# A range check's flag moved amid the last steps of an attention tail, with two banks for the turned sums and new scheduler settings

**Chip, cores, metric.** One core of one Trainium2 chip. The metric is the device time of one execution in microseconds (us); each comparison also runs the kernel before on the same chip.

## The reference

Two independent halves, written side by side into one output of 2048 x 1280 in bfloat16. The spectral half (A) multiplies a 2-d FFT by weights and transforms back. The attention half (B):

```python
H = 32; Dh = D // H                       # D = 640, Dh = 20, S = 2048
q, k, v = ...                             # from x @ wqkv
scores = jnp.einsum("bhqd,bhkd->bhqk", q, k) * Dh ** -0.5
p = _softmax(scores, axis=-1)
o = jnp.einsum("bhqk,bhkd->bhqd", p, v)
return (o, heads side by side) @ wo
```

## The kernel before

The kernel is made by a scheduler in Python. It walks through a simulated time with estimated durations (`occupy(engine, ns)`) and lays down one order of instructions for each engine. That order is then fixed; on the chip, semaphores decide when each instruction runs.

Attention is cut into 32 units (4 query blocks x 8 groups of 4 heads). Scores go by tiles of 128 x 512 through TensorE (PE). The exponentials are shared: ScalarE (ACT) takes groups of 3 and 2 tiles, VectorE (DVE) computes pairs of tiles by itself in 8 steps. The fast program skips the usual maximum of the softmax, so at its end it checks ranges (smallest and largest denominator, largest V) and makes a flag; every engine loads the flag and either jumps over a slow, safe program or runs it.

The V maxima, found as V is ready, and the last unit's steps (cut):

```python
def vmax(self):
    ...
    self.P.add("dve", lambda e: e.tensor_reduce(o, in_, AX.X, ALU.max, apply_absolute_value=True), ...)
    self.occupy("dve", 800.0)             # the scheduler's estimate

# tail_pe: turn the expanded reciprocals back by a matmul with the identity; all four in bank 4
    l, idf, o = self.rb[:, c], self.idf, ps[:, 4, c]
    self.P.add("pe", lambda e: e.matmul(o, l, idf, start=(qb == 0), stop=True, ...), ...,
               **({"w": [("ps", 4)]} if qb == 0 else {"pw": [("ps", 4)]}), name="tail_spread")
    ...
    ok = (qb == 0 or end) and (g == -1 or self.n_norm == 31)      # partial sums of the output projection

def tail_norm(self, qb):                  # normalise a quarter of the last unit
    b, osb, o = self.ps[:, 4, c], self.osb[:, c], self.OTn[:, NG - 1, c]
    self.P.add("dve", lambda e: e.tensor_tensor(o, osb, b, ALU.mult), ...)

def emit_flag(self):                      # called when all else is laid down
    # dve: csum (max over units), cv (max of V), f0, f1, f2 (comparisons)
    # pe: fsum (sum over partitions);  dve: fmin, flag

# every engine, at the end of its own list
    eng.wait_ge(flag semaphore)
    bad = eng.value_load(flag, min_val=0, max_val=3)
    with eng.If(bad > 0): ...             # the slow program
    # SyncE: wait for all output stores
```

Of the kernel before, what the change touches and what calls it, by code (L numbers as in the profile page):

```python
# [13 lines left out]
ALU = mybir.AluOpType  # L14
AX = mybir.AxisListType
# [218 lines left out]
NG = 8  # L234
# [1136 lines left out]
PE_LAT = 170.0  # L1371
# [13 lines left out]
class FK(KB):  # L1385
# [82 lines left out]
    def setup_B(self):  # L1468
        P = self.P
# [6 lines left out]
        kq[np.arange(128) % 32 < 20, 2] = 1.0  # L1476
        kqd = self.nc.inline_tensor(kq, self.prefix + "kq")
# [613 lines left out]
    def tail_pe(self):  # L2091
# [13 lines left out]
        for qb in range(4):  # L2105
            if self.tail_n.get(("e", qb), 1e18) <= self.now:
                del self.tail_n["e", qb]
                c = slice(qb * 128, (qb + 1) * 128)
                l, idf, o = self.rb[:, c], self.idf, ps[:, 4, c]
                self.P.add("pe", lambda e: e.matmul(o, l, idf, start=(qb == 0), stop=True, skip_group_check=True), r=[("rbl", qb), ("idf",)],  # L2110
                           **({"w": [("ps", 4)]} if qb == 0 else {"pw": [("ps", 4)]}), name="tail_spread")
                t = self.occupy("pe", self.pe_dur(300.0, "f"), PE_LAT)
                self.dve_urgent.append((t, lambda qb=qb: self.tail_norm(qb)))
                return True
# [16 lines left out]
        if self.tail_op:  # L2131
            qb, half, g = self.tail_op[0]
            ok = (qb == 0 or end) and (g == -1 or self.n_norm == 31)
            if qb == 0 and g == -1:

                bank = self.TAIL_BANK[0, half]
                ok = (self.u_act == 32 and self.x_pair is None and self.x_bank is None and not any(J.pe for J in self.jobs)
                      and self.bank_own.get(bank) is None and self.bank_t.get(bank, 0.0) <= self.now)
                if ok:
                    self.bank_own[bank] = "tail"  # L2140
            if ok:
                self.tail_op.pop(0)
                self.tail_mm(qb, half, g)
                return True
        return False

    def tail_rec(self):
        rin, rc, rb, ps = self.rin, self.rc, self.rb, self.ps
        P, mm = self.P, self.mm
# [3 lines left out]
        for h in range(2):  # L2153
# [5 lines left out]
            self.tail_n["e", 2 * h] = self.tail_n["e", 2 * h + 1] = t  # L2159
        self.now -= 800.0  # L2160
        m, both = mm[:, 62:64], self.rr.rearrange("p (c e) -> p c e", c=2)
        self.dve_urgent.append((self.now + 2000.0, lambda: (P.add("dve", lambda e: e.tensor_reduce(m, both, AX.X, ALU.max), r=[("rin",), ("rc",)], pw=[("mm",)], name="sums"), self.occupy("dve", 150.0))))
        self.at(self.now + 2000.0)

    def tail_norm(self, qb):
        c = slice(qb * 128, (qb + 1) * 128)
        b, osb, o = self.ps[:, 4, c], self.osb[:, c], self.OTn[:, NG - 1, c]
        self.P.add("dve", lambda e: e.tensor_tensor(o, osb, b, ALU.mult), r=[("osb",), ("ps", 4)], w=[("OTl", qb)], pw=[("OT", NG - 1)], name="tail_nrm")
        self.tail_n["n", qb] = self.occupy("dve", 270.0, 100.0)
# [141 lines left out]
    def vmax(self):  # L2311
# [8 lines left out]
        self.occupy("dve", 800.0)  # L2320
# [34 lines left out]
    def run(self):  # L2355
# [93 lines left out]
        self.emit_flag()  # L2449

    def emit_flag(self):
        P = self.P
        c, mm, fl = self.cert, self.mm, self.flagt
        ps = self.ps

        both = mm.rearrange("p (u c) -> p c u", c=2)
        P.add("dve", lambda e: e.tensor_reduce(c[:, 0:2], both, AX.X, ALU.max), r=[("mm",)], w=[("c", 0)], name="csum")
        P.add("dve", lambda e: e.tensor_reduce(c[:, 2:3], self.vmx, AX.X, ALU.max), r=[("vmx",)], w=[("c", 2)], name="cv")
        P.add("dve", lambda e: e.tensor_single_scalar(c[:, 3:4], c[:, 0:1], 65000.0, ALU.is_le), r=[("c", 0)], w=[("c", 3)], name="f0")
        P.add("dve", lambda e: e.tensor_single_scalar(c[:, 4:5], c[:, 1:2], 2.0 ** -6, ALU.is_le), r=[("c", 0)], w=[("c", 4)], name="f1")  # L2460
        P.add("dve", lambda e: e.tensor_single_scalar(c[:, 5:6], c[:, 2:3], 2.0 ** 60, ALU.is_le), r=[("c", 2)], w=[("c", 5)], name="f2")
        o1 = self.ones1
        P.add("pe", lambda e: e.matmul(ps[0:1, 7, 0:3], o1[:, 0:1], c[:, 3:6], start=True, stop=True),
              r=[("c", 3), ("c", 4), ("c", 5), ("ones1",)], w=[("ps", 7)], name="fsum")
        P.add("dve", lambda e: e.tensor_reduce(fl[0:1, 1:2], ps[0:1, 7, 0:3], AX.X, ALU.min), r=[("ps", 7), ("c", 5)], w=[("fl", 1)], name="fmin")
        fi = fl.bitcast(mybir.dt.int32)[0:1, 0:1]
        self.flag_task = P.add("dve", lambda e: e.tensor_single_scalar(fi, fl[0:1, 1:2], 127.5, ALU.is_lt), r=[("fl", 1)], w=[("fl", 0)], name="flag")
        self.flag = fi

# [8 lines left out]
def bass_concat_heads__spectral_gfnet__softmax_full_mha__prompt_kernel(  # L2478
# [11 lines left out]
    fast = FK(nc, arena, *args, cfg=dict(LEAD=32, T_A=600000.0, WARM_SHARE=0.43, RUN=1, PVQ=12, WIN=1400.0, T_X=30000.0, AHEAD=45e3, T_RB=9000.0, SKIP=0, ALONE=500.0, PVB=10, PTB=6, WARMUP=10))  # L2490
# [32 lines left out]
```

## Time and profile before

| | before |
|---|---|
| time, median of 6 runs | 858.4 us (857.6 to 858.7) |
| profiled execution | 856.3 us |
| first exponential starts | 10.50 us |
| last exponential ends | 841.35 us |
| last output add ends | 849.97 us |
| flag done | 851.02 us |

The span falls into the exponentials, where background work of half A and the projections is fitted in, and the tail behind them. The prediction shows the views of ScalarE and VectorE. TensorE's timeline of the tail shows the other partner (columns: start, length, engine, line, operation, operands, count, and in brackets the idle time before it and what ended it):

```profile
843.16 0.95 PE L2099 MATMUL ps<-arena 128*128 128x4 f32 x8
844.99 0.71 PE L2110 MATMUL ps<-arena 128*128 128x128 f32 x4
846.09 0.49 PE L2110 MATMUL ps<-arena 128*128 128x128 f32 x2 [0.38 <-DVE arena L2168]
846.95 0.49 PE L2110 MATMUL ps<-arena 128*128 128x128 f32 x2 [0.38 <-DVE arena L2168]
847.28 1.79 PE L2087 MATMUL ps<-arena 128*128 128x320 bf16 x12
```

L2099 sums the denominators, L2110 are the four turns, in fp32 (eight instructions in these rows, two for each turn), L2087 the twelve closing matmuls, in bf16 (one instruction each). The third turn waits for the first normalisation (0.38 us), the second normalisation waits for the third turn (0.58), the fourth turn waits for that (0.38): with its guard by bank, the kernel makes a ladder of the one bank. The output stores' line says how long they take from issue to landing:

```profile
DMA to landing us min/median/max: 1.8/1.9/1.9
```

### The profile page before, as it was taken

How to read it: one execution, taken by the hardware profiler on the slowest of the kernel's cores; microseconds unless marked ns; L12 is line 12 of the kernel's file. 1: busy time of each engine (PE TensorE's matmuls, PEld its weight loads, DVE VectorE, ACT ScalarE, POOL GpSimd, SP SyncE). 2: the span in 40 equal slices, each digit the busy share in tenths (PEclk: the TensorE clock that was granted, in tenths of full speed). 3: DMA queues.
4: the chain of work that ended last, by engine and by line, in shares of the span. 5: the costliest groups of instructions: out<-in, count | busy, mean ns of one | idle time of the engine just before them, and what ended most of it. 6: DMA issues, size and time to landing. Idle time of an engine off the chain costs nothing.

```text
span 856.3 us, 18371 instructions
## 1 busy us (share of the span) xinstructions
PE 796.4 (93%) x7802; PEld 277.2 (32%) x7828; DVE 760.6 (89%) x1475; ACT 830.3 (97%) x738; POOL 2.9 (0%) x8
## 2 busy tenths in 40 slices
PE   8999999999899999998899988888899999999995
PEld 4333323324223333332223432222333332333333
DVE  3577599999998999999998899999999889899983
ACT  6999999999999999999999999999999999999993
POOL 1000000000000000000000000000000000000000
PEclk9999999999999999999999999999999999999999
DMA  7520000000321000010101000001002111011201
GB/s 244 124 58 14 2 14 15 15 15 15 120 66 36 15 14 15 11 41 14 51 14 44 16 3 13 13 14 42 14 13 63 37 35 31 8 37 45 75 15 64
DMA packets 34461, 31.97 MB, mean 37 GB/s; under 512 B 13893, under 2 KB 28485, under 8 KB 34373
## 3 DMA queue, kind: packets, MB, share of 16 engines
q1 hardware_dynamic: 33796, 30.21, 11.7%
q8 instruction: 62, 1.02, 0.5%
q10 hardware_dynamic: 576, 0.52, 0.2%
q14 instruction: 27, 0.21, 0.1%
HBM read 24.97 MB, written 5.50 MB: 36 GB/s over the span
## 4 chain that ended last, share of the span: by engine, by line
ACT 56%; DVE 30%; PE 11%; issue 1%; POOL 0%; DVEq 0%; POOLq 0%
ACT arena L1783 56%; DVE arena L227 5%; DVE arena L1857 5%; PE ps L1766 3%; DVE arena L1253 3%; DVE arena L1897 2%; DVE arena L1901 2%; DVE arena L1525 2%; DVE arena L1904 2%; PE ps L1952 2%; PE ps L1581 2%; DVE arena L2318 1%; DVE arena L1893 1%; DVE arena L1895 1%; DVE arena L1899 1%
## 5 line engine op out<-in xcount | busy, mean ns | idle before, releaser
L1783 ACT ACTIVATE arena<-ps 128x1536 bf16<-128x1536 f32 x727 | 823.8, 1349 | 6.0 <-PE ps L1766 4.8
L1766 PE MATMUL ps<-arena 32*128 32x512 bf16 x2048 | 312.1, 384 | 35.6 <-ACT arena L1783 21.8
L1952 PE MATMUL ps<-arena 128*32 128x512 bf16 (+3 forms) x2048 | 192.9, 385 | 0.7 <-DVE arena L227 0.4
L1857 DVE TENSOR_SCALAR arena<-ps 128x512 uint16<-128x512 f32 x232 | 157.4, 684 | 10.2 <-PE ps L1766 9.8
L1766 PEld LDWEIGHTS ps<-arena 32*128 32x128 bf16 x2048 | 77.7, 91 | 268.5 <-ACT arena L1783 184.1
L227 DVE CAST arena<-ps 128x320 bf16<-128x320 f32 (+3 forms) x190 | 103.8, 546 | 25.0 <-PE ps L1610 11.5
L1901 DVE TENSOR_TENSOR arena<-arena 128x1024 f16<-128x1024 f16 x116 | 79.7, 687 | 1.0
L1897 DVE TENSOR_TENSOR arena<-arena 128x1024 f16<-128x1024 uint16 x116 | 79.5, 685 | 0.9
L1904 DVE TENSOR_TENSOR arena<-arena 128x1024 uint16<-128x1024 uint16 x116 | 79.3, 683 | 0.4
L1646 PE MATMUL ps<-arena 128*32 128x512 bf16 x808 | 75.4, 386 | 1.1 <-DVE arena L1972 1.1
L1952 PEld LDWEIGHTS ps<-arena 128*32 128x32 bf16 (+1 forms) x2048 | 47.4, 93 | 76.8 <-issue 63.3
L1525 DVE TENSOR_SCALAR arena<-ps,arena 128x512 bf16<-128x512 f32 x61 | 49.2, 806 | 23.6 <-PE ps L1581 14.3
L227 DVE COPY arena<-ps 128x1024 bf16<-128x1024 bf16 (+4 forms) x65 | 45.1, 697 | 14.1 <-PE ps L540 7.7
L1581 PE MATMUL ps<-arena 128*32 128x512 bf16 x640 | 53.1, 384 | 1.0 <-DVE arena L227 0.6
L1895 DVE TENSOR_SCALAR arena<-arena 128x1024 f16<-128x1024 uint16 x116 | 48.8, 421 | 1.0
L1662 PE MATMUL ps<-arena 128*32 128x512 bf16 x640 | 49.0, 382 | 0.6 <-DVE arena L227 0.4
L1893 DVE TENSOR_SCALAR arena<-arena 128x1024 uint16<-128x1024 uint16 x116 | 48.8, 421 | 0.7
L1899 DVE TENSOR_SCALAR arena<-arena 128x1024 f16<-128x1024 uint16 x116 | 48.9, 421 | 0.4
L1334 PE MATMUL ps<-arena 128*128 128x320 bf16 (+1 forms) x192 | 37.1, 302 | 0.0
L2032 PE MATMUL ps<-arena 128*128 128x320 bf16 x192 | 36.8, 302 | 0.3 <-DVE arena L227 0.3
L1610 PE MATMUL ps<-arena 128*128 128x80 bf16 (+1 forms) x320 | 32.2, 236 | 0.0
L1646 PEld LDWEIGHTS ps<-arena 128*32 128x32 bf16 x808 | 19.4, 93 | 39.1 <-issue 34.0
(74 smaller groups left out, 425.4 us busy)
## 6 DMA issues: line engine op xcount, KB each, us to landing
arena<-rscr SPq DMA_DIRECT2D x31, 256.0 KB
arena<-in_A_x_dram SPq DMA_DIRECT2D x4, 640.0 KB, 4.8
out_dram<-arena SPq DMA_DIRECT2D x4, 640.0 KB, 3.4
out_dram<-arena SPq DMA_DIRECT2D x15, 160.0 KB, 1.8
arena<-f_ciCS SPq DMA_DIRECT2D x8, 256.0 KB, 3.1
arena<-arena SPq DMA_DIRECT2D x124, 2.0 KB, 1.7
arena<-in_B_x_dram SPq DMA_DIRECT2D x3, 640.0 KB, 5.4
arena<-f_cslab SPq DMA_DIRECT2D x2, 768.0 KB, 5.2
```

The lines of the kernel that those rows point to most:

```text
L227: return eng.tensor_copy(out, in_)
L1525: return e.tensor_scalar(out, in_, m, b, ALU.mult, ALU.add)
L1581: inst = e.matmul(ps[32 * j:32 * j + 32, bank, :], self.wqkv[:, cbv, c:c + 32], r_, start=st, stop=sp, tile_position=(0, 32 * j))
L1646: i = e.matmul(ps[32 * j:32 * j + 32, 6, :], z, k, start=False, stop=False, skip_group_check=True, tile_position=(0, 32 * j))
L1766: inst = e.matmul(ps[:, bank, :], kt_[32 * j:32 * j + 32, g, kt * 128:(kt + 1) * 128], q[32 * j:32 * j + 32, :], start=True, stop=True, ti ...
L1783: self.P.add("act", lambda e: e.activation(pt, in_, AF.Exp, scale=SCALE, bias=-15.0 / LOG2E), r=[("ps", h + k) for k in range(n)], w=[("PT ...
L1857: self.P.add("dve", lambda e: e.tensor_scalar(v, in_, 1024.0 * SCALE * LOG2E, 31743.0, ALU.mult, ALU.min), r=[("ps", bank)], **({"w": [key ...
L1897: t = self.x_op(n, two, lambda e: e.tensor_tensor(b16, sh, b16, ALU.mult), [ka, kb], [kb], "x_q")
L1899: t = self.x_op(n, one, lambda e: e.tensor_scalar(a16, sh, -4.0 * X_B / 65536.0, -4.0 * X_A, ALU.mult, ALU.add), [ka], [ka], "x_l")
L1901: t = self.x_op(n, two, lambda e: e.tensor_tensor(b16, b16, a16, ALU.mult), [ka, kb], [kb], "x_h")
L1904: t = self.x_op(n, two, lambda e: e.tensor_tensor(v, v, b16, ALU.add), [kb, kv], [kv], "x_w")
L1952: inst = e.matmul(ps[32 * j:32 * j + m, 6, :], va[:, kt, 21 * h:21 * h + m], pt, start=st, stop=sp, tile_position=(0, 32 * j))
```

## The change

The intent: the flag's steps go where VectorE waits anyway, so that nothing follows the last output add; the turned sums alternate between banks 4 and 3, so that a turn and a normalisation can overlap; five settings are tuned anew. The diff, cut to its core:

```diff
+        kq[:, 4:6] = (65000.0, 2.0 ** -6)            # both limits as a tensor: one comparison for two
 # tail_pe
-                l, idf, o = self.rb[:, c], self.idf, ps[:, 4, c]
-                ... start=(qb == 0), stop=True, skip_group_check=True ... "w"/"pw": [("ps", 4)]
+                l, idf, o = self.rb[:, c], self.idf, ps[:, 4 - qb % 2, 0:128]
+                ... start=True, stop=True ... w=[("ps", 4 - qb % 2)]
+                if qb == 3:
+                    self.flag_mm()                     # now shifted by 300 around it
-            ok = (qb == 0 or end) and ...
+            ok = (qb == 0 or (end and self.tail_b is not None)) and ...
 # tail_rec, tail_norm
-            self.tail_n["e", 2 * h] = self.tail_n["e", 2 * h + 1] = t
+            if h == 0: self.tail_n["e", 0] = self.tail_n["e", 1] = t     # turns 2, 3 after norms 0, 1
+        self.flag_sums()                               # sums, csum, f0; occupy 560
+        if qb < 2: self.tail_n["e", qb + 2] = max(t, self.tail_e)
+        if qb == 3: self.flag_out()                    # fmin, flag; occupy 300
 # vmax
-        self.occupy("dve", 800.0)
+        self.occupy("dve", 760.0)
+        if kt == 15:
+            self.flag_v()                              # cv, f2; occupy 320
 # the end
-        self.emit_flag()
 # settings
-  T_A=600000.0, ... PVQ=12, ... T_X=30000.0, AHEAD=45e3, ... SKIP=0
+  T_A=560000.0, ... PVQ=10, ... T_X=25000.0, AHEAD=60e3, ... SKIP=2
```

More of the change, by code (lines that the diff above doesn't have):

```diff
@@ L2108, in tail_pe @@
                 c = slice(qb * 128, (qb + 1) * 128)
-                l, idf, o = self.rb[:, c], self.idf, ps[:, 4, c]
-                self.P.add("pe", lambda e: e.matmul(o, l, idf, start=(qb == 0), stop=True, skip_group_check=True), r=[("rbl", qb), ("idf",)],
-                           **({"w": [("ps", 4)]} if qb == 0 else {"pw": [("ps", 4)]}), name="tail_spread")
+                l, idf, o = self.rb[:, c], self.idf, ps[:, 4 - qb % 2, 0:128]
+                self.P.add("pe", lambda e: e.matmul(o, l, idf, start=True, stop=True), r=[("rbl", qb), ("idf",)],
+                           w=[("ps", 4 - qb % 2)], name="tail_spread")
                 t = self.occupy("pe", self.pe_dur(300.0, "f"), PE_LAT)
                 self.dve_urgent.append((t, lambda qb=qb: self.tail_norm(qb)))
+                if qb == 3:
+                    self.now += 300.0
+                    self.flag_mm()
+                    self.now -= 300.0
                 return True
@@ L2132, in tail_pe @@
             qb, half, g = self.tail_op[0]
-            ok = (qb == 0 or end) and (g == -1 or self.n_norm == 31)
+            ok = (qb == 0 or (end and self.tail_b is not None)) and (g == -1 or self.n_norm == 31)
             if qb == 0 and g == -1:
@@ L2148, in tail_rec @@
         rin, rc, rb, ps = self.rin, self.rc, self.rb, self.ps
-        P, mm = self.P, self.mm
+        P = self.P
         P.add("dve", lambda e: e.tensor_single_scalar(rin, ps[:, 2, 0:16], 1.0e-30, ALU.max), r=[("ps", 2)], w=[("rin",)], name="tail_max")
@@ L2158, in tail_rec @@
             t = self.occupy("dve", 350.0, 90.0)
-            self.tail_n["e", 2 * h] = self.tail_n["e", 2 * h + 1] = t
-        self.now -= 800.0
-        m, both = mm[:, 62:64], self.rr.rearrange("p (c e) -> p c e", c=2)
-        self.dve_urgent.append((self.now + 2000.0, lambda: (P.add("dve", lambda e: e.tensor_reduce(m, both, AX.X, ALU.max), r=[("rin",), ("rc",)], pw=[("mm",)], name="sums"), self.occupy("dve", 150.0))))
-        self.at(self.now + 2000.0)
+            self.tail_e = t
+            if h == 0:
+                self.tail_n["e", 0] = self.tail_n["e", 1] = t
+        self.now += 350.0
+        self.flag_sums()
+        self.now -= 1150.0
     def tail_norm(self, qb):
         c = slice(qb * 128, (qb + 1) * 128)
-        b, osb, o = self.ps[:, 4, c], self.osb[:, c], self.OTn[:, NG - 1, c]
-        self.P.add("dve", lambda e: e.tensor_tensor(o, osb, b, ALU.mult), r=[("osb",), ("ps", 4)], w=[("OTl", qb)], pw=[("OT", NG - 1)], name="tail_nrm")
-        self.tail_n["n", qb] = self.occupy("dve", 270.0, 100.0)
+        b, osb, o = self.ps[:, 4 - qb % 2, 0:128], self.osb[:, c], self.OTn[:, NG - 1, c]
+        self.P.add("dve", lambda e: e.tensor_tensor(o, osb, b, ALU.mult), r=[("osb",), ("ps", 4 - qb % 2)], w=[("OTl", qb)], pw=[("OT", NG - 1)], name="tail_nrm")
+        t = self.tail_n["n", qb] = self.occupy("dve", 270.0, 100.0)
+        if qb < 2:
+            self.tail_n["e", qb + 2] = max(t, self.tail_e)
+        if qb == 3:
+            self.now += 270.0
+            self.flag_out()
+            self.now -= 270.0
     def tail_add(self, qb, half):
@@ L2319, in vmax @@
                    r=[("V", kt, part) for part in range(4)] + [("Vones",)], pw=[("vmx",)], name="vmax")
-        self.occupy("dve", 800.0)
+        self.occupy("dve", 760.0)
+        if kt == 15:
+            self.now += 760.0
+            self.flag_v()
+            self.now -= 760.0
         return True
@@ L2448, in run, with flag_v @@
         self.sim_ns = self.now
-        self.emit_flag()
-    def emit_flag(self):
-        P = self.P
-        c, mm, fl = self.cert, self.mm, self.flagt
-        ps = self.ps
+    def flag_v(self):
+        c, vx = self.cert, self.vmx
+        self.P.add("dve", lambda e: e.tensor_reduce(c[:, 2:3], vx, AX.X, ALU.max), r=[("vmx",)], w=[("c", 2)], name="cv")
+        self.P.add("dve", lambda e: e.tensor_single_scalar(c[:, 5:6], c[:, 2:3], 2.0 ** 60, ALU.is_le), r=[("c", 2)], w=[("c", 5)], name="f2")
+        self.occupy("dve", 320.0)
@@ L2456, in emit_flag, with flag_sums @@
+    def flag_sums(self):
+        P, c, mm, rr, kq = self.P, self.cert, self.mm, self.rr, self.kq
         both = mm.rearrange("p (u c) -> p c u", c=2)
+        m, last = mm[:, 62:64], rr.rearrange("p (c e) -> p c e", c=2)
+        P.add("dve", lambda e: e.tensor_reduce(m, last, AX.X, ALU.max), r=[("rin",), ("rc",)], pw=[("mm",)], name="sums")
         P.add("dve", lambda e: e.tensor_reduce(c[:, 0:2], both, AX.X, ALU.max), r=[("mm",)], w=[("c", 0)], name="csum")
-        P.add("dve", lambda e: e.tensor_reduce(c[:, 2:3], self.vmx, AX.X, ALU.max), r=[("vmx",)], w=[("c", 2)], name="cv")
@@ L2459, in emit_flag @@
-        P.add("dve", lambda e: e.tensor_single_scalar(c[:, 3:4], c[:, 0:1], 65000.0, ALU.is_le), r=[("c", 0)], w=[("c", 3)], name="f0")
-        P.add("dve", lambda e: e.tensor_single_scalar(c[:, 4:5], c[:, 1:2], 2.0 ** -6, ALU.is_le), r=[("c", 0)], w=[("c", 4)], name="f1")
-        P.add("dve", lambda e: e.tensor_single_scalar(c[:, 5:6], c[:, 2:3], 2.0 ** 60, ALU.is_le), r=[("c", 2)], w=[("c", 5)], name="f2")
-        o1 = self.ones1
-        P.add("pe", lambda e: e.matmul(ps[0:1, 7, 0:3], o1[:, 0:1], c[:, 3:6], start=True, stop=True),
-              r=[("c", 3), ("c", 4), ("c", 5), ("ones1",)], w=[("ps", 7)], name="fsum")
@@ L2465, in emit_flag, with flag_mm @@
-        P.add("dve", lambda e: e.tensor_reduce(fl[0:1, 1:2], ps[0:1, 7, 0:3], AX.X, ALU.min), r=[("ps", 7), ("c", 5)], w=[("fl", 1)], name="fmin")
+        P.add("dve", lambda e: e.tensor_tensor(c[:, 3:5], c[:, 0:2], kq[:, 4:6], ALU.is_le), r=[("c", 0), ("kq",)], w=[("c", 3)], name="f0")
+        return self.occupy("dve", 560.0)
+    def flag_mm(self):
+        o1, c, ps = self.ones1, self.cert, self.ps
+        self.P.add("pe", lambda e: e.matmul(ps[0:1, 6, 0:3], o1[:, 0:1], c[:, 3:6], start=True, stop=True),
+                   r=[("c", 3), ("c", 5), ("ones1",)], w=[("ps", 6)], name="fsum")
+        self.occupy("pe", self.pe_dur(150.0, "f"), PE_LAT)
@@ L2466, in emit_flag, with flag_out @@
+    def flag_out(self):
+        P, fl, ps = self.P, self.flagt, self.ps
+        P.add("dve", lambda e: e.tensor_reduce(fl[0:1, 1:2], ps[0:1, 6, 0:3], AX.X, ALU.min), r=[("ps", 6)], w=[("fl", 1)], name="fmin")
         fi = fl.bitcast(mybir.dt.int32)[0:1, 0:1]
@@ L2468, in emit_flag @@
         self.flag = fi
+        self.occupy("dve", 300.0)
     def build(self):
@@ L2489, in bass_concat_heads__spectral_gfnet__softmax_full_mha__prompt_kernel @@
     arena = Arena(nc, 212832 - 64)
-    fast = FK(nc, arena, *args, cfg=dict(LEAD=32, T_A=600000.0, WARM_SHARE=0.43, RUN=1, PVQ=12, WIN=1400.0, T_X=30000.0, AHEAD=45e3, T_RB=9000.0, SKIP=0, ALONE=500.0, PVB=10, PTB=6, WARMUP=10))
+    fast = FK(nc, arena, *args, cfg=dict(LEAD=32, T_A=560000.0, WARM_SHARE=0.43, RUN=1, PVQ=10, WIN=1400.0, T_X=25000.0, AHEAD=60e3, T_RB=9000.0, SKIP=2, ALONE=500.0, PVB=10, PTB=6, WARMUP=10))
     fast.build()
```

## The prediction

> **What bounds the kernel now.** I read the page's slices and groups first, then busy time by stretch, then the timeline of the last 17 us, and last the instructions behind the flag. The groups say how long the exponentials on ScalarE (ACT) take, and how many score tiles VectorE (DVE) takes off it:
> ```profile
> L1783 ACT ACTIVATE arena<-ps 128x1536 bf16<-128x1536 f32 x727 | 823.8, 1349 | 6.0 <-PE ps L1766 4.8
> L1857 DVE TENSOR_SCALAR arena<-ps 128x512 uint16<-128x512 f32 x232 | 157.4, 684 | 10.2 <-PE ps L1766 9.8
> ```
> L1857 is the first step of the exponential that VectorE does by itself, in pairs of tiles. There are 2048 tiles (32 heads x 16 key blocks x 4 query blocks); VectorE takes 232, ScalarE the other 1816, at 823.8 / 1816 = 0.454 us each. It stands idle for only 6.0 us ahead of all 727 of them. The stretches (columns: stretch, its length, then busy us of PE, PEld, DVE, ACT and POOL, clock, DMA share, GB/s) say the same:
> ```profile
> 25.00:100.00 75.00, 73.39 (x881) 28.05 (x882) 48.21 (x82) 73.67 (x67) 0.29 (x1) 1.00 0.24 56
> 100.00:400.00 300.00, 285.44 (x2891) 96.69 (x2890) 290.43 (x566) 299.85 (x267) 0.00 (x0) 1.00 0.09 29
> 700.00:841.30 141.30, 134.68 (x1199) 45.61 (x1200) 126.29 (x253) 141.30 (x126) 0.00 (x0) 1.00 0.12 38
> ```
> From 100 to 400 us and from 700 us on, ScalarE is busy 100% of the time. So the time is three pieces: 10.5 us until the first exponential (it starts at 10.50 in ScalarE's timeline), some 831 us of exponentials to 841.3, and a tail of 15.0 us to the span's end at 856.3. Work moved between engines inside the middle piece changes nothing, unless it moves tiles between ScalarE and VectorE; an instruction saved in the tail counts in full, if it is on the tail's chain.
>
> The tail on VectorE and ScalarE, from the two timelines:
> ```profile
> 841.96 0.69 DVE L1972 COPY arena<-ps 128x512 f32<-128x512 f32 x1 [4.99 <-PE ps L1952]
> 844.15 0.18 DVE L2150 TENSOR_SCALAR arena<-ps 128x16 f32<-128x16 f32 x1 [1.49 <-PE ps L2099]
> 845.74 0.29 DVE L2168 TENSOR_TENSOR arena<-arena,ps 128x128 bf16<-128x128 f32 x1 [0.60 <-PE ps L2110]
> 846.61 0.29 DVE L2168 TENSOR_TENSOR arena<-arena,ps 128x128 bf16<-128x128 f32 x1 [0.58 <-PE ps L2110]
> 847.48 0.49 DVE L2168 TENSOR_TENSOR arena<-arena,ps 128x128 bf16<-128x128 f32 x2 [0.48 <-PE ps L2110]
> 848.29 1.68 DVE L2175 TENSOR_TENSOR arena<-ps,arena 128x320 bf16<-128x320 f32 x4 [0.33 <-PE ps L2087]
> 849.90 0.21 DVE L2457 TENSOR_REDUCE arena<-arena 128x2 f32<-128x64 f32 x1
> 850.47 0.19 PE L2463 MATMUL ps<-arena 128*1 128x3 f32 x2 [1.39 <-DVE arena L2461]
> 850.88 0.14 DVE L2467 TENSOR_SCALAR arena<-arena 1x1 int32<-1x1 f32 x1
> ```
> VectorE's steps here are short, and the bracket before nearly every one says that it waits for TensorE: the sums turned back (L2110) and the normalisation (L2168) take turns. The flag (L2457 to L2467) begins only where the last output add (L2175) ends, and ends at 850.88 + 0.14 = 851.02, 5.28 us ahead of the end. What those hold is in the lines of the flag's load, of the branch, and of the block's end:
> ```profile
> L178 DVEq TENSOR_LOAD <-arena x1: 543/543/543, 851.1 to 851.1; - x1
> L178 PEldq TENSOR_LOAD <-arena x1: 493/493/493, 851.1 to 851.1; - x1
> L179 PEldq COMPARE_BRANCH  x1: 4022/4022/4022, 851.9 to 851.9; - x1
> L168 ACTq DRAIN  x1: 80/80/80, 854.7 to 854.7; - x1
> L168 DVEq DRAIN  x1: 57/57/57, 855.3 to 855.3; - x1
> L168 PEldq DRAIN  x1: 63/63/63, 856.0 to 856.0; - x1
> ```
> All engines load the flag at the same moment and jump over the fallback program that is not run. From load to the drain behind the jump ScalarE takes 854.7 - 851.1 = 3.6 us, VectorE 4.2, TensorE 4.9; the last is the end, less 0.3 us of barrier.
>
> [...] The kernel does guard by bank: hence the waits of about 0.6 us above when all four turned sums share bank 4. [...] here 128x1 takes 0.14 us[...].
>
> **The change part by part.**
>
> First, the rest of qb=1's partial sums (an fp32 matmul) no longer stands ahead of the sum over the denominators (L2099) in TensorE's queue. The sum starts at 843.16; its input, the copy L1972, is there at 841.96 + 0.69 = 842.65. With 0.06 for the semaphore it could start at 842.71: 0.45 us earlier. But the fp32 pieces now stand behind it: the sum takes 0.81 us to issue (843.16 to 843.97), so to 843.52; then 0.53 + 0.13 + 0.53 if three of the four remaining steps come ahead of the turns, as the order of the scheduler's own estimates would have it: 844.73. VectorE's reciprocals are ready 0.45 us early, at 844.99 - 0.45 = 844.54. So the first turn starts at about 844.73, not 844.99. **Gain 0.25 us.**
>
> Second, two banks. Before, the first normalisation waits for two turns and each later one for a turn that itself waited for the one before. After: first turn 844.73 to 845.22 (0.49 us for its two instructions); VectorE does the last unit's sums, the maximum over all units and the comparison in the gap (0.18 + 0.21 + 0.15 us behind the expanding copy that ends 0.45 us earlier than 845.14, so 844.69 to about 845.25); first normalisation 845.26 (before 845.74), second 845.48 (846.61), turns 3 and 4 from 845.6 and 845.8, normalisations 3 and 4 about 846.14 and 846.36, done 846.65 (before 847.97). [...] Hence the first add starts about 848.29 - 1.09 = 847.20. The flag's last two steps (0.15 + 0.14 us, L2465 and L2467) fit before it, at 846.65 to 846.97. **Gain at the adds about 1.1 us, the first step's 0.25 included.** The adds themselves remain 1.68 us: VectorE ends at 848.88 and not at 849.97.
>
> Third, nothing is behind the adds any more: the flag is there at about 846.97, and each engine loads and jumps once its own work is over. TensorE: last matmul done about 848.0, plus 4.9, is 852.9. VectorE: 848.88 + 4.2 = 853.1. ScalarE: the last store is issued at 848.93 to 849.28 (before 850.01 to 850.36), plus 3.6, is 852.9. SyncE has to see the last store land, 1.9 us after its issue: 850.8, not on the path. Plus 0.3 for the barrier: end 853.4, 2.9 us ahead of 856.3. Of that, 1.1 is the turns and 1.8 the flag. I take **2.8 us**, as the reducing of the V maxima (0.16 + 0.14 us) moves into the middle on VectorE, where it costs next to nothing.
>
> Fourth, the settings. T_X = 25 us for 30 lets VectorE begin its tiles sooner; AHEAD = 60 for 45 us forces the K and V projections sooner; T_A = 560 for 600 us paces the spectral half faster; SKIP = 2 lets a VectorE tile pass two groups that use its rows; PVQ = 10 for 12 gates background work. All this only counts by tiles moved. One pair more on VectorE takes 2 x 0.454 = 0.91 us from ScalarE and costs VectorE 2 x 0.684 + 3 x 0.421 + 3 x 0.685 = 4.7 us. VectorE stands idle for 75 - 48.2 = 26.8 us between 25 and 100 us and for about 15 us after 700 us, so there is room for some pairs. But TensorE is busy for 73.4 of those 75 us and the projections hold the two spare banks there, and more projections forced early makes that worse. I can't work out the schedule by hand; a setting chosen anew is likelier to help. My choice: two pairs, **1.8 us**, from one pair lost to five gained.
>
> Sum: 858.3 - 2.8 - 1.8 = 853.7 us.
>
> **The rivals.** (a) The jump sets the end whatever happens: if the instruction fetches behind it, not the flag's value, are the limit and do not begin sooner, or if TensorE's 4.0 us become longer when output stores are still under way, the third step gives 0.5 us in place of 1.8: about 855.0. For it: the 4022 ns are unlike the 50 to 72 ns of the other engines' branch. Against: each engine's load stands right behind the flag (851.1 after 851.02). (b) The flag's steps amid the tail delay it: the chain L2162-L2457-comparison ahead of the first normalisation is as long as the gap, and if each dependent step costs 0.2 us plus a semaphore, the normalisations lose 0.2 to 0.4 us: about 854.0. (c) The settings hurt or help more than thought: VectorE kept off tiles by the new rule of SKIP, or TensorE congested before 100 us, gives about 856; five pairs gained gives about 851. This is the largest doubt, as nothing in the profile bounds it but VectorE's idle time.
>
> **Range and chances.** The tail's gain is 2.2 to 3.3 us, the settings' -1 to 4.5; together I hold 850.8 to 856.6 for 8 in 10. Two per cent would be 17 us, more than the whole tail of 15.0 us or than 18 pairs of tiles: faster by over 2% has a chance of 0.01, slower by over 2% 0.01 as well.
>
> **What would show each step right or wrong.** The denominators' sum should start within 0.1 us of the end of the last copy. The second normalisation should start some 0.2 us after the first, with no wait of 0.58 us ahead of it. The flag should be ready before the first output add, and the engines' loads of it should no longer stand at one moment, with VectorE's right behind its last add. From the end of the last exponential to the end of the span there should be about 12.1 us, not 15.0. Count the VectorE tiles: 236 against 232 is my guess, and 0.454 us a tile is what a different count is worth. I am wrong if the end keeps 5 us behind the last add plus a second wait, or if the exponentials' piece (10.5 to 841.3) moves by over 4 us either way.

In the trace of before an fp32 matmul of 128x320 is two instructions 0.269 us apart, so 0.538 us, and a bf16 one 0.136; put in for 0.53 and 0.13 in the first step they give the same 844.73. (The 0.06 for the semaphore is 0.05 there, from the end of the first normalisation at 846.03 to the third turn at 846.09.) The 1.09 us of the second step is the forecast move of the closing matmuls, which started at 847.28, to a place behind the flag's matmul at about 846.2.

## The result

The change takes 856.88 us in the median of 6 runs (855.87 to 860.6), the kernel before 858.4. The ratio is 0.9989 (0.9971 to 1.0007): no difference is established by these runs. (A ratio is the mean of one kernel's fast runs over the mean of the other's of the same rounds, so not quite the ratio of the medians quoted.) The gain that was forecast, 4.6 us, did not come; by the medians 1.5 us of it may have. The change's runs also spread more (855.9 to 860.6 us against 857.6 to 858.7); the section on the settings comes back to that.

The tail did what was forecast. VectorE's timeline of the kernel after:

```profile
843.26 0.69 DVE L1973 COPY arena<-ps 128x512 f32<-128x512 f32 x1 [1.93 <-PE ps L1953]
846.00 0.18 DVE L2477 TENSOR_REDUCE arena<-arena 128x2 f32<-128x32 f32 x1
846.47 0.16 DVE L2479 TENSOR_TENSOR arena<-arena 128x2 f32<-128x2 f32 x1
846.63 0.51 DVE L2174 TENSOR_TENSOR arena<-arena,ps 128x128 bf16<-128x128 f32 x2
847.50 0.51 DVE L2174 TENSOR_TENSOR arena<-arena,ps 128x128 bf16<-128x128 f32 x2 [0.36 <-PE ps L2111]
848.11 0.14 DVE L2492 TENSOR_SCALAR arena<-arena 1x1 int32<-1x1 f32 x1
848.77 1.68 DVE L2187 TENSOR_TENSOR arena<-ps,arena 128x320 bf16<-128x320 f32 x4 [0.52 <-PE ps L2088]
```

The normalisations (L2174) come in two pairs without the ladder's waits, the flag (L2492) is done at 848.25, and the last add ends at 850.45 with nothing behind it. TensorE, of the same kernel:

```profile
844.00 1.05 PE L2100 MATMUL ps<-arena 128*128 128x4 f32 x8
846.21 0.61 PE L2111 MATMUL ps<-arena 128*128 128x128 f32 x4
846.98 0.71 PE L2111 MATMUL ps<-arena 128*128 128x128 f32 x4
847.74 1.80 PE L2088 MATMUL ps<-arena 128*128 128x320 bf16 x12
```

The sum (L2100) starts 0.05 us behind the copy's end (843.95). From the last exponential's end (842.75) to the end of the span (854.87) there are 12.1 us, where before had 15.0: the forecast was 12.1 (that it is met to a tenth is luck, as point 4 of the account below says). The loads of the flag, the branches and the drains now stand apart:

```profile
L178 PEldq TENSOR_LOAD <-arena x1: 484/484/484, 848.9 to 848.9; - x1
L178 ACTq TENSOR_LOAD <-arena x1: 623/623/623, 850.9 to 850.9; - x1
L179 PEldq COMPARE_BRANCH  x1: 4122/4122/4122, 849.8 to 849.8; - x1
L168 PEldq DRAIN  x1: 63/63/63, 853.9 to 853.9; - x1
L168 ACTq DRAIN  x1: 82/82/82, 854.5 to 854.5; - x1
L168 SPq COMPARE_BRANCH  x1: 38/38/38, 854.5 to 854.5; - x1
```

TensorE jumps while VectorE still adds (its branch starts at 849.8 us, the last add ends at 850.45). ScalarE, which issues the last store, is now last (3.6 us from load to drain, as before), together with SyncE, which I had not expected; its own waits and the stores' landings say why:

```profile
SPq L191 <- DMA out_dram<-arena: 2.6, 2, 2.3
DMA to landing us min/median/max: 1.8/3.9/4.0
```

SPq L191 is SyncE's wait for the output stores (us in total, times, longest). The stores now take twice as long to land as before (3.9 us and not 1.9), at the same moment as packets on the instruction queues, which I take for the jumps' fetches. The packets in the trace say how: of the last store's 144 packets, 135 have ended by 853.0 us and the last nine only after 853.5, while packets of 8 and 16 KB run on two instruction queues (850.3 to 853.3 us). In the kernel before all 144 had ended by 851.6, and the instruction packets began at 852.7.

So the gain went in the middle. The groups of the kernel after (columns: busy us, mean ns of one, idle us of the engine just before and what ended most of it):

```profile
L1784 ACT ACTIVATE arena<-ps 128x1536 bf16<-128x1536 f32 x726 | 824.2, 1354 | 6.2 <-PE ps L1767 5.1
L1858 DVE TENSOR_SCALAR arena<-ps 128x512 uint16<-128x512 f32 x234 | 158.7, 682 | 9.1 <-PE ps L1767 8.9
```

VectorE takes one pair more (234 tiles and not 232), so ScalarE has 1814 tiles and not 1816. Yet its busy time grew from 823.8 to 824.2 us, and its stretch of exponentials from 830.9 us (10.50 to 841.35) to 831.5 us (11.29 to 842.75). The start itself came 0.8 us later.

**Where "100% busy" misleads.** I read the start times of single exponentials out of the traces. In the kernel before, a group of three tiles is followed by the next start after 1.331 us in the median, a group of two after 0.904 us: 2.235 us for five tiles, 0.447 us each. No step is shorter (the least are 1.330 and 0.904), so that is the floor. Ten groups in the early part run at it: 11.40 us, which is 5 x 2.235 and the run-out of the last. But 56 of the groups of two are followed late, by over 0.06 us each and 15.1 us in all (2.2 us of it around another instruction of ScalarE, at 18.1 us, which takes 0.8 us itself). An instruction's recorded length (1.14 us for two tiles) is longer than its step by 0.23 us, so the first 0.23 us of each such delay show no idle time. The stretch less 0.447 us per tile is the wait in all, shown or not, but for that instruction's 0.8 us and the last one's run-out of 0.2: 830.85 - 1816 x 0.447 = 19.1 us before, of which the group's row shows 6.0. For the other kernels the same sum is in the table of the next section.

### The profile page after: what moved, and what is told of

Its sections match the earlier page's. It is cut to its first block, busy times and chain, and to the rows that moved or that the text cites. A ratio compares the mean times of both kernels' runs of the same rounds, so it can differ in the third digit from the quotient of the medians.

```text
span 854.9 us, 18317 instructions
## 1 busy us (share of the span) xinstructions
PE 793.8 (93%) x7767; PEld 278.6 (33%) x7794; DVE 761.8 (89%) x1482; ACT 830.8 (97%) x737; POOL 2.9 (0%) x8
## 4 chain that ended last, share of the span: by engine, by line
ACT 55%; DVE 32%; PE 12%; issue 1%; DVEq 0%; POOL 0%; POOLq 0%
ACT arena L1784 55%; DVE arena L227 6%; DVE arena L1858 5%; PE ps L1767 3%; DVE arena L1253 3%; DVE arena L1902 3%; DVE arena L1898 2%; DVE arena L1905 2%; DVE arena L1526 2%; PE ps L1953 2%; PE ps L1582 2%; DVE arena L1894 2%; DVE arena L1896 1%; DVE arena L1900 1%; DVE arena L2330 1%; PE ps L1611 1%
## 5 line engine op out<-in xcount | busy, mean ns | idle before, releaser
L1784 ACT ACTIVATE arena<-ps 128x1536 bf16<-128x1536 f32 x726 | 824.2, 1354 | 6.2 <-PE ps L1767 5.1
L227 DVE CAST arena<-ps 128x320 bf16<-128x320 f32 (+3 forms) x190 | 103.5, 545 | 30.8 <-PE ps L2033 12.4
L1647 PE MATMUL ps<-arena 128*32 128x512 bf16 x772 | 72.0, 386 | 1.3 <-DVE arena L1973 1.3
L1582 PE MATMUL ps<-arena 128*32 128x512 bf16 x640 | 52.2, 383 | 0.9 <-DVE arena L227 0.6
L1663 PE MATMUL ps<-arena 128*32 128x512 bf16 x640 | 48.1, 382 | 0.0
L1170 PE MATMUL ps<-arena 128*128 128x328 bf16 x160 | 32.7, 306 | 0.3 <-DVE arena L227 0.3
```

The costliest lines, as they stand in the source:

```text
L227: return eng.tensor_copy(out, in_)
L1582: inst = e.matmul(ps[32 * j:32 * j + 32, bank, :], self.wqkv[:, cbv, c:c + 32], r_, start=st, stop=sp, tile_position=(0, 32 * j))
L1647: i = e.matmul(ps[32 * j:32 * j + 32, 6, :], z, k, start=False, stop=False, skip_group_check=True, tile_position=(0, 32 * j))
L1784: self.P.add("act", lambda e: e.activation(pt, in_, AF.Exp, scale=SCALE, bias=-15.0 / LOG2E), r=[("ps", h + k) for k in range(n)], w=[("PT ...
```

## The experiments

Twelve runs, all correct. They ran on two chips, each with its own runs of the kernel before (medians 858.2 to 858.4 us): tail_same_middle, tail_only, settings_only and after_again on the one, the other eight on the other. First the table that they add up to. "Pairs" is VectorE's; "waits" is the stretch of exponentials less 0.447 us for each of ScalarE's tiles; "tail" goes from the last exponential's end to the end of the span. All three are from the profile, one execution; "time" is the median of 5 or 6 runs, "ratio" that to the kernel before in the same rounds, with an interval of about 0.0013 (1.1 us) to each side, and up to 0.0018 for the change.

| kernel | pairs | first exp. | waits | tail | time | ratio |
|---|---|---|---|---|---|---|
| before | 116 | 10.50 | 19.1 | 15.0 | 858.4 | 1 |
| the change | 117 | 11.29 | 20.6 | 12.1 | 856.88 | 0.9989 |
| after_again | 117 | 10.93 | 21.1 | 12.2 | 856.78 | 0.9990 |
| tail_same_middle | 116 | 10.68 | 19.4 | 12.4 | 855.98 | 0.9973 |
| tail_only | 114 | 10.67 | 20.6 | 12.5 | 859.49 | 1.0020 |
| settings_only | 116 | 10.21 | 18.9 | 15.2 | 858.61 | 1.0009 |
| estimate_alone | 118 | 11.11 | 20.1 | 17.8 | 860.83 | 1.0033 |
| flagv_estimate_alone | 117 | 10.57 | 22.8 | 12.4 | 858.74 | 1.0006 |
| skip2_old_estimate | 116 | 10.56 | 18.6 | 12.6 | 856.02 | 0.9971 |
| after_two_dummies | 117 | 10.40 | 29.2 | 12.2 | 864.82 | 1.0079 |

But for after_two_dummies the program is the same in all of these for its first 130 us, yet the first exponential comes anywhere from 10.2 to 11.3 us. So the 0.8 us later start in the change's profile is scatter of the run, and differences between two profiles below that are read here from their parts, not from their ends.

### What of the settings is alive

Before the experiments I built the change with four of the five settings put back (T_A, PVQ, T_X, AHEAD) and compared its instructions with those of the change, engine by engine: they are the same. This is a comparison of built programs and not a run. It gave files that are the same byte for byte; so did the kernel before with SKIP = 2 alone against settings_only.

Four of the five settings change nothing at all; only SKIP does. What I had not seen is that the two estimates do: 760 for 800 ns for each of 16 V maxima, and 320 ns for the V part of the flag. From the first V maxima on (137 us in the trace of before) the scheduler's clock runs otherwise, and the whole middle gets another order.

### tail_same_middle: the tail alone

```diff
-        self.occupy("dve", 760.0)
+        self.occupy("dve", 800.0)
         if kt == 15:
             self.flag_v()              # its two steps, without an estimate
-  ... the new settings
+  ... the settings of before
```

> The tail and flag of the change alone: the settings of before, and the scheduler is given its old estimate (800 ns) for the V maxima and none for the two small flag steps put behind them, so that the order of instructions on every engine is that of before until the tail, with 116 VectorE pairs and 727 exponentials, but for two steps of 0.15 us. Theory A (the tail gained its 2.8 us and the reshuffled middle gave 1.4 us back): 858.4 - 2.8 = 855.6 us, ratio 0.9967, and 12.1 us from the last exponential's end to the end of the span. Rival B (the tail's gain is not real in the timed runs, or depends on the new middle): 856.9 to 858.4 us.

Measured 855.98 us (855.61 to 856.2), ratio 0.9973 (0.996 to 0.9986): 2.3 us gained on the kernel before, with an interval that excludes equality; the whole change had 0.9989 and no such certainty. The order on all engines up to the tail is that of before, but for the two small steps. Theory A stands: the tail gained, and something else in the change gave back. Its 2.8 us were a little too much: the profile's tail is 12.4 us and not 12.1. And the two small steps, put into the middle, are not quite free: in the trace they run at 196.5 us, and from the exponentials near 204 to 207 us on this kernel is 0.35 us behind the kernel before, each measured from its own first exponential. It is so in all six profiles that have these steps in the old middle (0.36 to 0.40 us); 0.27 us of it is left at the end of the stretch. So the profile has 2.6 us gained in the tail, less 0.3 in the middle: the 2.3 us of the timed runs.

### tail_only, settings_only and after_again: estimates and settings apart

```diff
 tail_only:      the change with T_A=600000, PVQ=12, T_X=30000, AHEAD=45e3, SKIP=0
 settings_only:  the kernel before with T_A=560000, PVQ=10, T_X=25000, AHEAD=60e3, SKIP=2
 after_again:    the change itself
```

> The change with all five settings put back. The program the scheduler then makes has 114 VectorE pairs and 728 exponentials: the shorter estimate for the V maxima alone reshuffles the middle. Theory A: the tail as in the change (12.1 us), two pairs fewer than before cost 2 x 0.91 us in the middle: 855.6 + 1.8 = 857.4 us. Rival C (the number of pairs doesn't decide, the waits between exponentials do): anything from 855 to 859, not in line with the count.

Measured 859.49 us: slower than the kernel before, with the better tail. Against tail_same_middle only the two estimates differ, and they cost 3.5 us: of this the profile shows 3.0 as two pairs fewer (2 x 2 x 0.447 = 1.8 us) and 1.2 us more waits. The forecast by pairs alone (857.4) was 2 us short, so rival C has its share.

> The kernel before with the five new settings and nothing else: 116 pairs and 727 exponentials as before, the order of TensorE and VectorE changed from about unit 9 on. Theory A: same count, so 858.4 us within 0.5. Rival C (waits between exponentials decide): off by 1 us or more either way. Tail 15.0 us in either case.

Measured 858.61 us (857.4 to 861.0), ratio 1.0009 (0.9996 to 1.0021): nothing gained by the settings alone, as A expected from the count. The runs' spread is new, and so is their mean granted clock: 0.995 in three runs, 0.998 and 0.989 in the others, the last being the slowest at 861.0 us. The stretches of the profiled run show a low window (columns as in the prediction; the third from the end is the granted clock):

```profile
620.00:625.00 5.00, 4.28 (x46) 1.87 (x42) 4.79 (x6) 5.00 (x5) 0.00 (x0) 1.00 0.16 56
625.00:630.00 5.00, 3.89 (x36) 0.93 (x33) 4.90 (x10) 4.59 (x5) 0.00 (x0) 0.88 0.00 0
630.00:635.00 5.00, 5.00 (x39) 1.87 (x35) 4.20 (x9) 3.73 (x4) 0.00 (x0) 0.78 0.17 52
635.00:640.00 5.00, 4.75 (x52) 1.45 (x48) 5.00 (x11) 5.00 (x6) 0.00 (x0) 1.00 0.02 5
```

After the stretch in which TensorE had the least to do (3.89 us of 5) its clock is low, and ScalarE, which waits for its scores, is busy only 3.73 us of the next 5. In the trace's clock record the low stretch is 3.41 us at half clock, from 628.84 us on. TensorE was not idle before it: in the 3.41 us before the fall it was busy for 2.30.

Two more profiles have such a window (after_again at 643.98 us, flagv_estimate_alone at 622.27), with TensorE busy for 2.54 and 2.29 of the 3.41 us before it. But skip2_old_estimate has a stretch of 2.30 us too (at 626.1, counted back in steps of 3.413 us from its low clock at the end of the span, as the windows above lie 65, 61 and 68 such steps before theirs; the full-clock stretches of the kernel before and of the change, 849.92 and 846.51 us in their clock records, are 249 and 248 of them), and no fall: little work (2.29 to 2.54 us of 3.41) stands before each of the three falls, and doesn't settle whether one comes. What a window costs can be read from pairs with the same order in the middle. settings_only loses 1.2 us at once against skip2_old_estimate, and 0.8 of it is left at the last exponential; after_again loses 0.8 us against the change, and 0.5 is left.

> The whole change again, for comparison on this chip. 117 pairs and 726 exponentials. Measured before: 856.9 us. Its first exponential came at 11.29 us and not 10.50, though the first 130 us of the program are those of before: if that is jitter of the run, it will be near 10.5 in some of the profiles of these four. By the count of pairs it should be 855.6 - 0.9 = 854.7 us; by the waits between exponentials 856.9 us again.

Measured 856.78 us (855.66 to 861.22), as before. Its two slowest runs over both sets (860.6 and 861.22 us) are those with the lowest clock, 0.990; those at 0.998 or 0.999 took 855.66 to 857.09 us. So SKIP = 2 on top of the estimates gains 2.7 us (859.49 to 856.78), which is what three pairs are worth (114 to 117: 3 x 0.9), while SKIP = 2 on the old order gains nothing in the timed runs. Against tail_same_middle this profile has +0.25 us at the start, -0.9 us of tiles, +1.7 us of waits, -0.2 us of tail: 0.9 us in all, as the spans differ (855.1 and 854.2). About 0.5 us of these waits is the window at half clock; the change's first profile, without one, has 1.2 us more waits than tail_same_middle.

### one_bank_order, one_bank, partials_first, flag_at_end: the parts of the tail

All four start from tail_same_middle, whose order in the middle they share.

```diff
 one_bank_order:  turns into ps[:, 4, c] again, released as before when the copies are there
 one_bank:        turns into ps[:, 4, c] again, order of instructions unchanged
 partials_first:  ok = (qb == 0 or end) and ...
 flag_at_end:     flag_sums, flag_mm, flag_out called after all else (flag_v stays)
```

> The kernel tail_same_middle (856.0 us; 12.4 us from the last exponential's end to the end of the span) with the turned sums back in one bank and turns three and four released as before, when the copies are there. All else of the change stays. Theory A (the false wait of a normalisation for the next turn is worth what the chain showed: first normalisation 0.3 us later behind two turns, second 0.6 us later): last add 0.7 to 0.9 us later, 856.8 us, tail 13.1 to 13.3 us. Rival (TensorE's closing matmuls or the flag's place set the adds): under 0.3 us.

> The kernel tail_same_middle with the turned sums in one bank and nothing else: each engine's order of instructions stays that of the change, so the second normalisation no longer waits for the third turn; but the third turn now waits for the second normalisation as well, and the first normalisation for one turn or two. Theory A: 0.2 to 0.5 us, 856.3 us, tail 12.6 to 12.9 us; so most of the two banks' gain would be the order. Rival: the same 0.7 to 0.9 us as in one_bank_order.

> The kernel tail_same_middle with the guard taken out that holds back qb=1's partial sums until the sum over the denominators is issued. Theory A (my step one): the sum starts 0.45 us later, but one fp32 partial fewer stands between it and the turns: 0.2 us later in all, tail 12.6 us, 856.2 us. Rival: no difference, as TensorE does the same work before the first turn in either order, and only its start counts: 12.4 us.

> The kernel tail_same_middle with the flag's steps behind the output adds again (the V part stays in the middle): sums, maximum, comparison, matmul, minimum, flag. Theory A: 1.8 us later, as the engines' loads of the flag wait for it and the jump of TensorE (4.0 us) starts only then: 857.8 us, tail 14.2 us. Rival (the jump ends when it ends, or SyncE's wait for the last store sets the end): under 1 us.

From the profiles, in us (copy: end of the last unit's copy; add: end of the last output add):

| kernel | copy to add | add to end | time | ratio |
|---|---|---|---|---|
| before | 7.32 | 6.33 | 858.4 | 1 |
| tail_same_middle | 6.50 | 4.6 | 855.98 | 0.9973 |
| one_bank_order | 6.86 | 4.1 | 856.32 | 0.9976 |
| one_bank | 6.93 | 4.3 | 856.6 | 0.9983 |
| partials_first | 6.75 | 4.6 | 856.88 | 0.9982 |
| flag_at_end | 6.27 | 6.2 | 857.68 | 0.9994 |

The two banks are worth 0.36 us at the adds (0.43 with the order of the change), half of what I expected; the waits of the ladder are back (VectorE, one_bank_order):

```profile
847.03 0.29 DVE L2173 TENSOR_TENSOR arena<-arena,ps 128x128 bf16<-128x128 f32 x1 [0.45 <-PE ps L2111]
847.90 0.68 DVE L2173 TENSOR_TENSOR arena<-arena,ps 128x128 bf16<-128x128 f32 x3 [0.58 <-PE ps L2111]
```

but the three last normalisations then run together (0.68 us for three), so the ladder has one rung only. At the end of the span nothing is left: both columns together are 11.0 us (one_bank_order) and 11.2 (one_bank) against 11.1, as the stores of the later adds land sooner (3.6 us, not 4.1). In the times (0.3 and 0.6 us) the difference is inside the intervals. one_bank, expected at 0.2 to 0.5 us, shows 0.43 at the adds; that it would be better than one_bank_order isn't so.

partials_first gives 0.25 us at the adds, the number of my first step, but not by its path. The sum does start 0.45 us later there (0.50 and not 0.05 us behind the copy's end), yet the first turn only 0.07 us later (2.34 and 2.26), as TensorE has less to do between the two. What moves the adds is the first normalisation (2.95 and 2.69): in both kernels it starts just behind VectorE's comparison for the flag, and VectorE's steps are 0.35 us later. (This is read from the two traces; no run separates it.) In time it is 0.9 us slower than tail_same_middle, but the ratios' intervals overlap.

flag_at_end is the largest part. The adds end 0.23 us sooner relative to the copy, so the flag's steps amid the tail do cost that. They don't cost it at the first normalisation, which starts 2.69 us behind the copy's end in both kernels; the flag's matmul stands ahead of the closing ones, and these start 0.21 us later than without it (3.79 and 3.58 us behind the copy's end). Against it stand 1.6 us behind the adds, so 1.4 us in all (a tail of 13.8 us and not 12.4). The timed runs have 1.7 us, more than the 1.4 but within their intervals. The stores, issued at the same distance from the adds as in tail_same_middle, land faster again; the branches start at 851.6 to 851.7 us here, when the last store, issued at 849.7, has just landed:

```profile
DMA to landing us min/median/max: 1.8/1.9/1.9
```

In tail_same_middle the same line has 1.9/4.1/4.1, with TensorE's branch from 848.9 to 853.2 us and the last store issued at 849.7. So the early jumps do slow the stores, and take back part of what they bring. In tail_same_middle SyncE's wait for the last store ends within 0.2 us of ScalarE's jump, so to shorten one alone would bring little; that was not tried.

### estimate_alone and flagv_estimate_alone: the estimates one by one

```diff
 estimate_alone:        tail_same_middle with self.occupy("dve", 760.0) for the V maxima
 flagv_estimate_alone:  tail_same_middle with self.occupy("dve", 320.0) for the V part of the flag
```

> The kernel tail_same_middle with the scheduler's estimate for the V maxima at 760 and not 800 ns: no instruction is added or taken away by that, only the order changes from about 135 us on. The program has 118 VectorE pairs (two more) and 725 exponentials, and the last steps of the spectral half move behind the exponentials. By the count of pairs: 856.0 - 1.8 = 854.2 us. Theory C (waits between exponentials, hidden in ScalarE's busy time, and what is left behind the exponentials decide, and a new order is a new draw): 2 us or more off that, most likely slower.

Measured 860.83 us (860.03 to 862.21): 4.9 us slower than tail_same_middle with two pairs more. The stretch of exponentials did get shorter (830.0 us), but half A's last steps are left behind it, and the tail has 17.8 us. ScalarE's timeline shows two of nine of them:

```profile
842.40 0.43 ACT L226 CAST arena<-ps 128x320 bf16<-128x320 f32 x1 [0.83 <-PE ps L1334]
851.63 0.43 ACT L226 CAST arena<-ps 128x320 bf16<-128x320 f32 x1 [0.39 <-PE ps L1334]
```

> The kernel tail_same_middle with the 320 ns estimate for the V part of the flag and no other change: 117 pairs, 726 exponentials. By the count 855.1 us; by theory C anything within 3 us of 856. If it is within 0.5 us of 855.1 the count is not refuted here.

Measured 858.74 us: 3.6 us off the count's 855.1, so the count is refuted here. The waits are 22.8 us, 3.4 more than in tail_same_middle, and the group's row shows all of that as idle time (10.0 us against 6.0):

```profile
L1784 ACT ACTIVATE arena<-ps 128x1536 bf16<-128x1536 f32 x726 | 822.7, 1344 | 10.0 <-PE ps L1767 9.1
```

A window at half clock lies in this profile, but it does not explain the loss: the run with the highest clock (0.999) still took 858.12 us.

The two estimates cost 4.9 and 2.8 us alone and 3.5 us together. They are not additive: each is a new order, with its own pairs, waits and leftovers.

### skip2_old_estimate and after_two_dummies: SKIP and the clock

```diff
 skip2_old_estimate:  tail_same_middle with SKIP=2
 after_two_dummies:   the change, with self.dummy2() called twice in warm(), occupied once
```

> The kernel tail_same_middle with SKIP = 2, the only one of the five settings that changes the program: 116 pairs, as without. By the count 856.0 us. settings_only, with the same middle, was at 858.6 against 858.2 us, with a granted clock of 0.995 in most runs: theory D (some orders let TensorE fall to half clock for a window of 3.4 us, and each one costs about 1 us) expects 856.4 us in the median, a spread of 3 us or more, and the slow ones at the lower clock.

Measured 856.02 us (854.72 to 856.39), ratio 0.9971: as fast as tail_same_middle, to the expected count. The expected spread of 3 us did not come (1.7 us, clock 0.996 to 0.999), though settings_only, with the same middle, had it (857.4 to 861.0 us, clock 0.989 to 0.998). So the low clock is not a property of the order alone; the two kernels also ran on different chips, which these runs don't separate.

> The whole change with every warming matmul in the middle doubled, without time for it in the scheduler's plan (some 220 matmuls of 0.21 us on TensorE, where it had little to do). Theory D (the loss against 855.7 us in the change's runs is windows at half clock, after too little work on TensorE): clock at least 0.998 in all runs, spread under 1.5 us, median 855.9 us. Rival: the extra matmuls delay the scores: slower by 1 us or more at any clock; or the windows at half clock come anyway.

The clock was 0.999 to 1.0 in all runs and the spread 1.1 us, where the change had 0.990 to 0.999 and 4.7 us: that agrees with theory D, but the share of work at which the clock falls was not shown. But the time was 864.82 us: the 221 extra warming steps (of one or four matmuls each, 800 matmuls, more than I had counted) delay the scores, and the waits are 29.2 us. The rival is right about the price. As the other engines' orders are those of the change, it also shows that work on TensorE, which no view calls the bound, is paid in ScalarE's waits: 8.6 us more than in the change's profile (29.2 - 20.6), of which the group's row shows 4.7 as idle time (10.9 us against 6.2).

Two kernels have the best medians, tail_same_middle and skip2_old_estimate, at 856.0 us: the change without its new estimates. They are faster than the kernel before by intervals that exclude equality (0.9960 to 0.9986 and 0.9958 to 0.9985); against the change (0.9973 to 1.0008 in after_again's rounds) the intervals overlap.

## Why the prediction was wrong

1. **First step, the sum ahead of the partials: right in number, partly by luck.** 0.25 us forecast, 0.25 us measured at the adds (partials_first). The sum starts 0.45 us sooner, as forecast; but the first turn was to gain the 0.25 us, and gained 0.07. By the traces the adds gained the rest because VectorE's flag steps, which the change puts ahead of the first normalisation, run sooner too.
2. **Second step, two banks: right in kind, too large.** The adds end 0.82 us sooner behind the copy (7.32 to 6.50), not 1.1 us. The first normalisation starts 2.69 us behind the copy's end and not 2.61 (845.26 - 842.65), as TensorE needs 0.2 us longer from the sum to the first turn; the flag's steps amid the tail take 0.23 us. The banks' own share is 0.36 us.
3. **Third step, the flag off the end: right.** 1.8 us forecast; 6.3 to 4.6 us behind the add, and 1.6 us when undone (flag_at_end), less the 0.23 us of point 2. One sign was missed: VectorE's load was to stand right behind its last add, and it starts at 849.6 us, 0.8 us before that add ends (850.45): the load does not wait for the adds to end. What ends last was not as forecast: I had VectorE's jump last and SyncE "not on the path" with a landing of 1.9 us. It is ScalarE's jump together with the last store, which lands after 3.9 us.
4. **The sum of the tail: 2.8 us forecast, 2.6 in the profile (15.0 to 12.4), 2.3 in the timed runs** (tail_same_middle). The change's own 12.1 us came as forecast by luck: 0.11 us of its distance from 12.4 is a shorter way from the last exponential to the copy in its order (1.20 and 1.31 us), the rest a sooner end behind the adds. The reducing of the V maxima, which I took for "next to nothing" in the middle, costs 0.3 us there, which is the step from 2.6 to 2.3.
5. **Fourth step, the settings: failed.** The step that failed is "My choice: two pairs, 1.8 us", and under it the view that "all this only counts by tiles moved". One pair came and not two (234 tiles, not 236), and its 0.9 us was lost to waits between the exponentials, which grew by 1.5 us (19.1 to 20.6). Against tail_same_middle, which has the tail alone, the settings and estimates together lose 0.8 to 0.9 us in the medians; that loss is within the noise, but a gain of 1.8 us is not. I took five settings for alive, of which four change no instruction. I took the estimate's change from 800 to 760 ns for nothing, and gave the V part "next to nothing": as instructions they cost 0.3 us (tail_same_middle holds them), as estimates they redraw the order and cost 3.5 us. SKIP then gave back 2.7 us. I had also taken 0.454 us a tile as ScalarE's cost; 0.447 is its cost and the rest is waits, which a new order can change by as much as the count is worth.
6. **The rivals.** (a) was wrong as put (the jumps do begin sooner), though it named the stores. (b) had the size (0.2 us) and not the place. (c), "the settings hurt", is nearest to what happened, through a cause that I had not named: the estimates hurt, and SKIP, taken alone, shows no loss.
7. **What remains open:** which of the reordered instructions cause the added waits. The runs show that the order decides, not which step of it. The profiles narrow down where: from the same group to the same group, the change is level with tail_same_middle up to 127 us and 1.75 us behind it by 297 us (group 250), and from there to the last groups it stays 0.9 to 1.8 us behind. Why the granted clock of settings_only's runs (0.989 to 0.998) was below that of skip2_old_estimate's (0.996 to 0.999), with the same middle but for the two small steps, isn't settled either.

## What to carry to other kernels

In a kernel laid down by a scheduler, a change of one estimate is a change of the program: compare the built orders first, and test a local change with the rest of the order held still, or its gain and a lucky or unlucky redraw can't be told apart. An engine that shows 100% can still be waiting (before, ScalarE showed it from 700 to 841 us, while 19.1 us of waits lay in the stretch of exponentials, some 12 of them not shown as idle); compare the step from start to start with its best value. And when several engines must jump at the end, let each begin as soon as its own work is done, but count the jumps against the last stores. Here the branch on TensorE took 3.8 to 4.6 us in all profiles and ScalarE needed 3.4 to 3.8 us from load to drain; output stores under way at the same time landed after 3.9 us (the change), 4.1 (tail_same_middle) and 3.5 (one_bank_order) in the median, and after 1.9 in flag_at_end and the kernel before.
